# Attention weights sent between tiles on chip in 8 transfers per unit, instead of through DRAM

## The chip, the cores and the metric

The kernel runs on one core of a Trainium2 chip. The metric is the device time of one execution in microseconds (us). The kernel before took 1465.52 us, the median of three runs (1459.74 to 1465.77).

## The reference

Two blocks follow each other. The first is attention with a threshold, over 8 batches, 8 heads, 576 rows and a head size of 64, all float32. The second is a bilinear feed-forward layer over 4608 rows of 512 with 1536 hidden columns.

```python
scores = scale * np.matmul(q, k.transpose(0, 1, 3, 2))
thresh = np.max(scores, axis=-1, keepdims=True) - tau
scores = np.where(scores >= thresh, scores, -1000000000.0)
scores = scores - np.max(scores, axis=-1, keepdims=True)
attn = np.exp(scores)
attn = attn / (np.sum(attn, axis=-1, keepdims=True) + 1e-09)
out = np.matmul(attn, v)
# (B,H,S,D) -> (B*S, H*D) = x
a = x @ w_a
b = x @ w_b
return (a * b) @ w_out
```

## The kernel before

**Units.** Heads are taken in pairs: 8 batches of 4 pairs (HP = 4), 32 pairs. A pair's 576 query rows make five units: u = 0 to 3 are 128 rows for both heads, u = 4 (NT) is the tail of 64 rows, where both heads share one 128-row tile. That makes 160 units. The list `units` (L895 to L903) orders them: per batch first the units 0 and 1 of all four pairs, then 2, 3 and the tail of each; the first batch (i < HP) has its tails last.

**Slots.** The loop at L925 runs one slot per unit. In slot g TensorE computes the scores of unit g (`scores`, L340), VectorE (DVE) takes their maxima, ScalarE (ACT) the exponentials, DVE applies the threshold and sums (`weigh`), and ACT normalises (`normalise`). The result is the tile tw (three buffers): 128 partitions with query rows, and per head 576 keys in 18 blocks of 32.

**Turning the weights.** The product with v contracts over keys, so keys must lie on partitions. The first 8 units (BY_PE) are turned by TensorE (`turn_pe`). For the others DVE transposes tw in place in 32x32 blocks (`turn_blocks`, L446), in slot g + 1. After that the partition group of 32 still belongs to one block of 32 queries, and holds one key of each of the 18 key blocks, for both heads. To bring different keys to different groups, four transfers write the groups to DRAM (swap, L457), and in the slot after, `turn_back` reads it back in one transfer (L466; two at L469 for the later tails) into a tile wT, of which there are two. Partitions 0 to 63 then hold keys of the first head, 64 to 127 of the second.

**Product.** `weighted` (L539) runs for a part of a pair: units 0 and 1 (256 queries) or units 2, 3 and the tail (320 queries); in the first batch the tails are parts of their own. It runs PV_LAG = 3 slots after the part's last unit. `product` (L476) issues 36 matmuls over nine slots of keys, two row groups (one per head) by two column groups; results of a head lie crosswise in two PSUM banks, so `settle` (L487) copies one bank by ACT in one instruction and the other by DVE in two halves across partitions.

**The feed-forward layer** fills the rest of each slot: `advance` steps through its matmuls (L633, L706, L763) by a count of columns owed, `make_room` moves a product to where an accumulation ends. TensorE's instructions stand in the order of the program.

**Loads.** SyncE's queue (SP) issues nearly all transfers, in the program's order: k, q (L147) and v (L170, L172) of later pairs, weights in the first slots (L225), the swaps, and the stores of the output (L833). Eight semaphores are used in turn for its transfers, and a transfer waits for the landing of the one eight places before it.

## Time and profile before

| What | Value |
|---|---|
| median of three runs | 1465.52 us |
| profiled execution | 1467.37 us |
| its span on the core | 1465.6 us |
| TensorE clock granted | 0.994 of full |
| TensorE / DVE / ACT / GpSimd busy | 95 / 69 / 47 / 33% |
| bytes moved by DMA | 223.21 MB, 60.7% of 16 engines' time on SP's queue |
| busy of TensorE, 0 to 146.6 us | 111.2 of 146.6 us |
| busy of TensorE, 146.6 to 1330 us | 1146.9 of 1183.4 us |
| busy of TensorE, 1330 us to the end | 129.8 of 135.6 us |
| DMA share in these (first 73.3 us / to 146.6 / middle / end) | 1.06 / 0.69 / 0.66 / 0.05 |

Three stretches can be told apart. At the start loads fill the transfer engines and weights are converted. In the middle attention and feed-forward layer share the slots. After the last product, at 1330 us, only the feed-forward layer of the last rows is left. A group's line in the profile names the source line, the engine, the operation, the tiles out<-in, the shape and the count; after the bar come busy time, the mean duration of one in ns, and the idle time of the engine just before these instructions with what ended most of it. In a list of waits the numbers are us in total, times, and the longest. In a list of transfers they are the count, the size of one and the median us from issue to landing. A line of the timeline starts with start and duration in us.

### The profile page before, as it was taken

What the parts mean: (1) busy time and instruction counts of PE and PEld (TensorE: products, weight loads), DVE (VectorE), ACT (ScalarE), POOL (GpSimd) and SP (SyncE); (2) the same over time, 40 slices, a digit from 0 to 9 for tenths busy, and PEclk for the clock granted to TensorE, in tenths of its full rate; (3) what the DMA queues carried; (4) which work ended last, traced back from release to release, by engine and by line L of the source; (5) the groups of instructions that cost most, each with busy time, mean ns of one, the idle gap of its engine ahead of it and who ended that gap; (6) DMA issues with size and microseconds to landing.
All of it is one profiled execution on the core that took longest, in us unless ns stands there. A gap on an engine that the chain in (4) does not pass through costs nothing.

```text
span 1465.6 us, 76332 instructions
## 1 busy us (share of the span) xinstructions
PE 1387.9 (95%) x34208; PEld 1248.2 (85%) x34208; DVE 1014.9 (69%) x2245; ACT 682.9 (47%) x1243; POOL 479.5 (33%) x668
## 2 busy tenths in 40 slices
PE   5788999999999999999999899999999999999998
PEld 4677687987989889899998788998898979989997
DVE  6898688787767787586757677767767776755223
ACT  5787455545545554454444445444545455431110
POOL 2774713423060606033334224150606060605000
PEclk9999999999999999999999999999999999999999
DMA  9976677668756775577555766477656776450000
GB/s 217 227 207 181 155 183 190 167 169 189 195 135 160 165 203 145 137 174 180 142 135 138 163 165 169 121 177 167 173 147 144 179 188 165 122 148 30 4 17 17
DMA packets 325080, 223.21 MB, mean 152 GB/s; under 512 B 169616, under 2 KB 308880, under 8 KB 324752
## 3 DMA queue, kind: packets, MB, share of 16 engines
q1 hardware_dynamic: 322384, 217.73, 60.7%
q8 instruction: 269, 4.41, 1.3%
q10 hardware_dynamic: 2368, 0.59, 0.2%
q14 instruction: 59, 0.48, 0.1%
HBM read 128.58 MB, written 89.65 MB: 149 GB/s over the span
## 4 chain that ended last, share of the span: by engine, by line
PE 78%; DVE 7%; DMA 5%; SPq 5%; issue 3%; ACT 1%; POOL 1%; ACTq 0%; DVEq 0%; POOLq 0%
PE pab L633 24%; PE pab L706 18%; PE po L763 17%; PE pv L483 9%; PE sc L352 9%; DMA wT<-swap 2%; SPq L457 2%; DVE mx L359 2%; SPq L147 1%; DMA qT<-in_q_dram 1%; DVE tw L446 1%; DVE tw L383 1%; PE po L809 1%; SPq L225 1%; POOL kept L732 0%
## 5 line engine op out<-in xcount | busy, mean ns | idle before, releaser
L402 ACT ACTIVATE tw<-tw,rcp 128x576 f32<-128x576 f32 x272 | 197.8, 769 | 216.9 <-DVE rcp L396 216.8
L359 DVE TENSOR_REDUCE mx<-sc 128x1 f32<-128x576 f32 x288 | 205.6, 751 | 134.6 <-PE sc L352 131.3
L380 ACT ACTIVATE tw<-sc,bias,scalars 128x576 f32<-128x576 f32 x288 | 239.3, 831 | 9.8 <-DMA vm<-in_v_dram 0.2
L599 POOL TENSOR_TENSOR h<-h,u 128x512 f32<-128x512 f32 x28 | 35.1, 1272 | 621.8 <-DVE h L676 485.8
L383 DVE SCALAR_TENSOR_TENSOR tw<-sc,thr,tw 128x576 f32<-128x576 f32 x288 | 223.0, 798 | 14.0 <-ACT tw L380 13.8
L763 PE MATMUL po<-wo_sb,h 64*64 64x256 f32 x3264 | 222.9, 377 | 0.0
L352 PE MATMUL sc<-kT,qT 64*64 64x288 f32 x2016 | 192.0, 405 | 10.5 <-ACT xt L490 4.7
L446 DVE STREAM_TRANSPOSE tw<-tw 128x576 f32<-128x576 f32 x272 | 196.0, 754 | 0.8 <-ACT tw L402 0.8
L483 PE MATMUL pv<-wT,vm 64*64 64x160 f32 (+3 forms) x5184 | 182.4, 275 | 14.3 <-DMA wT<-swap 8.0
L763 PEld LDWEIGHTS po<-wo_sb,h 64*64 64x64 f32 x3264 | 167.4, 133 | 24.9
L483 PEld LDWEIGHTS pv<-wT,vm 64*64 64x64 f32 x5184 | 166.2, 135 | 25.3 <-issue 10.4
L763 PE MATMUL po<-sums_u,h 64*64 64x256 f32 x2448 | 163.9, 376 | 1.6 <-DVE h L714 1.6
L732 POOL TENSOR_TENSOR h<-h 128x256 f32<-128x256 f32 x168 | 117.4, 728 | 114.6 <-PE po L763 100.5
L352 PEld LDWEIGHTS sc<-kT,qT 64*64 64x64 f32 x2016 | 115.1, 133 | 32.5 <-ACT xt L490 12.3
L763 PEld LDWEIGHTS po<-sums_u,h 64*64 64x64 f32 x2448 | 123.4, 133 | 20.7 <-DVE h L714 2.3
L633 PE MATMUL pab<-xU,wb_sb 64*64 64x128 f32 x4096 | 133.5, 270 | 0.2 <-issue 0.2
L379 ACT ACTIVATE bias<-mx,scalars 128x1 f32<-128x1 f32 x288 | 83.0, 288 | 100.6 <-DVE mx L359 100.5
L633 PEld LDWEIGHTS pab<-xU,wb_sb 64*64 64x64 f32 x4096 | 127.6, 133 | 2.6 <-issue 0.5
L491 DVE COPY xT<-pv 64x128 f32<-64x128 f32 (+1 forms) x136 | 38.1, 280 | 120.3 <-PE pv L483 119.1
L633 PE MATMUL pab<-xS,wa_sb 64*64 64x128 f32 x2048 | 110.8, 270 | 3.2 <-POOL xS L506 2.0
L490 ACT COPY xT<-pv 128x128 f32<-128x128 f32 (+1 forms) x68 | 17.6, 258 | 206.0 <-PE pv L483 205.9
L706 PE MATMUL pab<-xS,wb_sb 64*64 64x256 f32 (+1 forms) x1536 | 99.9, 359 | 2.9 <-issue 2.9
(137 smaller groups left out, 2429.0 us busy)
## 6 DMA issues: line engine op xcount, KB each, us to landing
swap<-tw SPq DMA_DIRECT2D x480, 144.0 KB, 2.6
wT<-swap SPq DMA_DIRECT2D x120, 576.0 KB, 4.7
vm<-in_v_dram SPq DMA_DIRECT2D x128, 72.0 KB, 3.3
swap<-tw SPq DMA_DIRECT2D x128, 72.0 KB, 2.0
kT<-in_k_dram SPq DMA_DIRECT2D x112, 72.0 KB, 4.3
wT<-swap SPq DMA_DIRECT2D x56, 144.0 KB, 2.9
out_dram<-kept SPq DMA_DIRECT2D x30, 256.0 KB, 4.0
qT<-in_q_dram SPq DMA_DIRECT2D x112, 40.0 KB, 4.5
```

What stands on the lines that cost most here:

```text
L352: nc.tensor.matmul(sc[j if u < NT else 0][to, c], qT[r, q0:q0 + D], kT[r, c * SH:(c + 1) * SH], start=True, stop=True)
L359: nc.vector.tensor_reduce(mx[:, c], sc[j], axis=AX.XY, op=ALU.max)
L379: nc.scalar.activation(bias[:, j:j + 1], mx[:, j:j + 1], AF.Copy, scale=e_nscale)
L380: nc.scalar.activation(wb[j], sb[j], AF.Exp, bias=bias[:, j:j + 1], scale=e_scale)
L383: nc.vector.scalar_tensor_tensor(out=wv, in0=sb[j], scalar=thr[:, j:j + 1], in1=wv, op0=ALU.is_ge, op1=ALU.mult, accum_out=sums[:, j:j + 1])
L402: nc.scalar.activation(w, w, AF.Copy, scale=rcp[:, j:j + 1])
L446: nc.vector.transpose(w, w)
L483: nc.tensor.matmul(pv[c * D:(c + 1) * D, y], vm[rows, s], wT[y](rows, s), start=(s == 0), stop=(s == NSLOT - 1))
L633: nc.tensor.matmul(out[c * D:(c + 1) * D, r, f * P:(f + 1) * P], w[g][k][rows, w0:w0 + D], moving[k][rows], start=(fresh and k == 0 and f ...
L706: nc.tensor.matmul(pab[c * D:(c + 1) * D, r], w[rows, f // n, k, fs + c * D:fs + (c + 1) * D], moving, start=(k == 0), stop=(k == H - 1))
L732: (nc.vector if state["over"] else nc.gpsimd).tensor_tensor(*a, **kw)
L763: nc.tensor.matmul(po[c * D:(c + 1) * D, r, y], ht[rows, t0:t0 + D], other[rows, f], start=(f == 0), stop=(f == NF // 2 - 1))
```

## The change

The weights no longer pass through DRAM. `turn_blocks` only transposes; `send` then copies the transposed groups from tw straight into wT, in eight transfers per unit, one per group of 32 query rows and half of the keys. The new wT holds a whole part (two heads, up to five column groups), and there is one of it instead of two of half the size. `send_ready` holds the units that wait for it: the first unit of a part is sent only after the product of the part before has been issued, and its transfer waits for that product to have read the tile.

In the new layout a row group of 64 partitions holds keys for its own query blocks, for both heads, instead of one head for all queries. So v must lie in both row groups for both heads: `load_part` loads it once per part, in four transfers of twice the size (eight transfers with rows of 64 elements in the first batch), into one of two tiles. `load_v` stays for the first eight units. `product_of` keeps the number and shapes of the matmuls; a head's result now lies in one partition half in both banks, so that ACT copies one bank and DVE the other with one instruction each, in strides. The product runs PV_LAG = 2 slots after the part's last unit. The first eight units' turned weights use the two halves of the one wT tile.

```diff
-PV_LAG = 3
+PV_LAG = 2
...
+    def load_part(i, h):
+        b, hp = pairs[i]
+        vm = loads.tile([P, 2, NSLOT, D], FP32, tag="vm", bufs=2, name="vm")
+        vms[i, h] = vm
+        both = v[b, 2 * hp:2 * hp + 2]
+        for g in range(G):
+            to = vm[g * Q:(g + 1) * Q]
+            if i >= HP:
+                nc.sync.dma_start(to.rearrange("p j s d -> p j (s d)"),
+                                  both.rearrange("j (p c s) d -> c p j (s d)", p=Q, c=2)[g % 2])
             else:
+                for j in range(2):
+                    nc.sync.dma_start(to[:, j], both[j].rearrange("(c s p) d -> c p s d", c=2, p=Q)[g % 2])
...
     def turned_tile():
-        return work.tile([P, G + 1, NSLOT, Q], FP32, tag="wT", bufs=2, name="wT")
+        return work.tile([P, 2, G + 1, NSLOT, Q], FP32, tag="wT", bufs=1, name="wT")
...
     def turn_blocks(i, u):
         ws, _ = weights.pop((i, u))
-        t = whole.pop((i, u))
         for w in ws:
             nc.vector.transpose(w, w)
-        if u < NT:
-            swap = scratch.tile([G, P, NSLOT * Q], FP32, tag="swap", name="swap")
-        else:
-            swap = scratch.tile([2, P, NSLOT * Q], FP32, tag="swapt", name="swap")
-        swaps[i, u] = swap
+
+    def send(i, u):
+        t = whole.pop((i, u)).rearrange("p (j c s) e -> p j c (s e)", j=2, c=2)
+        wT = turned[i, 0].rearrange("p j g s e -> p j g (s e)")
         for g in range(G):
-            if u < NT:
-                to, n = swap[g], G
-            else:
-                to, n = swap[g % 2, (1 - g // 2) * D:(2 - g // 2) * D], 2
-            nc.sync.dma_start(to.rearrange("(r p) e -> p r e", p=Q),
-                              t[g * Q:(g + 1) * Q, 0:n * NSLOT].rearrange("p (r s) e -> p r (s e)", r=n))
-
-    def turn_back(i, u):
...
+            for c in range(2):
+                rows = t[g * Q:(g + 1) * Q]
+                if u < NT:
+                    r = g // 2
+                    nc.sync.dma_start(wT[(2 * r + c) * Q:(2 * r + c + 1) * Q, :, u % 2 * 2 + g % 2], rows[:, :, c])
+                else:
+                    r, j = g % 2, 1 - g // 2
+                    nc.sync.dma_start(wT[(2 * r + c) * Q:(2 * r + c + 1) * Q, j, G if i >= HP else i], rows[:, 0, c])
+
+    def send_ready():
+        while ready:
+            i, u = ready[0]
+            if (i, 0) not in turned:
+                if turned:
+                    return
+                turned[i, 0] = turned_tile()
+                for p in range(HP if u == NT else 0):
+                    turned[p, 0] = turned[i, 0]
+            send(*ready.pop(0))
...
+    def product_of(wT, vm):
+        pv = banks(wT.shape[2] * Q, "pv")
+        for s in range(NSLOT):
+            for r in range(2):
+                rows = slice(r * D, (r + 1) * D)
+                for c in range(2):
+                    nc.tensor.matmul(pv[c * D:(c + 1) * D, r], vm[rows, c, s], wT[rows, c, :, s],
+                                     start=(s == 0), stop=(s == NSLOT - 1))
+        return pv
...
     def weighted(i, h):
...
+            x = x_of[b, h][:, hp].rearrange("p (u r w) -> p u r w", u=2, r=2)
+            main = pv[:, :, 0:P].rearrange("p r (u w) -> p r u w", u=2)
+            read[0].append(nc.scalar.copy(x[:, :, 0], main[:, 0]))
+            read[1].append(nc.vector.tensor_copy(x[:, :, 1], main[:, 1]))
...
+            x = xtail_of[b // GT][:, hp, t * TAIL:(t + 1) * TAIL].rearrange("p (r w) -> p r w", r=2)
+            tail = pv[:, :, pv.shape[2] - Q:]
+            read[0].append(nc.scalar.copy(x[:, 0], tail[:, 0]))
+            read[1].append(nc.vector.tensor_copy(x[:, 1], tail[:, 1]))
...
         if g > BY_PE and g <= len(units):
             turn_blocks(*units[g - 1])
+            ready.append(units[g - 1])
+        if g > BY_PE:
+            send_ready()
...
                 weighted(*part(*units[n]))
                 running["owed"] -= NSLOT * width(*part(*units[n])) // 2
-            if BY_PE + 1 < g <= len(units) + 1:
-                turn_back(*units[g - 2])
+                done = parts.index(part(*units[n])) + 1
+            send_ready()
...
-        for p in range(1, NPR):
+        for p in range(1, HP):
             if g == first[p] - 1:
                 load_v(p)
-        if BY_PE <= g < BY_PE + HP:
-            load_v(g - BY_PE, again=True)
+        if g in (BY_PE - 1, BY_PE + 1):
+            load_part(*parts[g > BY_PE])
+        if done and done + 1 < len(parts):
+            load_part(*parts[done + 1])
```

More of the change, by code (lines that the diff above doesn't have):

```diff
@@ L122 @@
     small = pool("small", 2)
-    scratch = pool("scratch", 3, space=bass.MemoryType.DRAM)
     psum = pool("psum", 4, space=PSUM)
@@ L156, in load_rows, with load_v @@
         loaded.setdefault(i, {})[name] = room
-    def load_v(i, again=False):
+    def load_v(i):
         b, hp = pairs[i]
-        if not again:
-            loaded[i]["v"] = loads.tile([P, NSLOT, D], FP32, tag="vm", bufs=HP, name="vm")
+        if i % 2 == 0:
+            state["v"] = loads.tile([P, 2, NSLOT, D], FP32, tag="vm", bufs=2, name="vm")
+        loaded[i]["v"] = state["v"][:, i % 2]
         for j in range(2):
-            rows, half = v[b, 2 * hp + j], loaded[i]["v"][j * D:(j + 1) * D]
-            if i >= HP or again:
-                if i < HP:
-                    rows = rows.rearrange("(c s p) d -> p c s d", c=2, p=Q)
-                else:
-                    rows = rows.rearrange("(p c s) d -> p c s d", c=2, p=Q)
-                for c in range(2):
-                    nc.sync.dma_start(half[c * Q:(c + 1) * Q], rows[:, c])
-            else:
-                nc.sync.dma_start(half, rows.rearrange("(s p) d -> p s d", p=D))
+            nc.sync.dma_start(loaded[i]["v"][j * D:(j + 1) * D], v[b, 2 * hp + j].rearrange("(s p) d -> p s d", p=D))
+    def load_part(i, h):
[8 more added lines that the diff above has]
+                                  both.rearrange("j (p c s) d -> c p j (s d)", p=Q, c=2)[g % 2])
+            else:
+                for j in range(2):
+                    nc.sync.dma_start(to[:, j], both[j].rearrange("(c s p) d -> c p s d", c=2, p=Q)[g % 2])
     CW = DM
@@ L198 @@
     state = {"loaded": 0, "added": 0, "converted": 0, "rows": 0, "sums": False, "through": 0, "over": False,
-             "layer": False, "reading": False, "first": 0}
+             "layer": False, "v": None, "reading": False, "first": 0}
     NSUM = NF // 2 * 3 * CH
@@ L314 @@
     x_of, xtail_of = {}, {}
-    blocks, complete, swaps = [], [], {}
+    blocks, complete, vms, ready = [], [], {}, []
     def prep(i, name):
@@ L419, in turn_pe @@
         ws = [w.rearrange("p n e -> p (n e)") for w in ws]
-        wT = turned_tile()[:, 0:G].rearrange("p g s e -> p (g s e)").rearrange("p (s w) -> p s w", w=P)
+        if "pe" not in turned:
+            turned["pe"] = turned_tile()
+        wT = turned["pe"][:, units.index((i, u)) % 2, 0:G].rearrange("p g s e -> p (g s e)")
+        wT = wT.rearrange("p (s w) -> p s w", w=P)
         turned[i, u, "pe"] = [wT[:, :, y * D:(y + 1) * D] for y in range(2)]
@@ L443, in turn_blocks @@
         ws, _ = weights.pop((i, u))
-        t = whole.pop((i, u))
         for w in ws:
             nc.vector.transpose(w, w)
-        if u < NT:
-            swap = scratch.tile([G, P, NSLOT * Q], FP32, tag="swap", name="swap")
-        else:
-            swap = scratch.tile([2, P, NSLOT * Q], FP32, tag="swapt", name="swap")
-        swaps[i, u] = swap
-        for g in range(G):
-            if u < NT:
-                to, n = swap[g], G
-            else:
-                to, n = swap[g % 2, (1 - g // 2) * D:(2 - g // 2) * D], 2
-            nc.sync.dma_start(to.rearrange("(r p) e -> p r e", p=Q),
-                              t[g * Q:(g + 1) * Q, 0:n * NSLOT].rearrange("p (r s) e -> p r (s e)", r=n))
-    def turn_back(i, u):
-        swap = swaps.pop((i, u)).rearrange("g p e -> p g e")
-        if u < NT or i < HP:
-            turned[i, u] = turned_tile()
-            n = G if u < NT else 2
-            nc.sync.dma_start(turned[i, u][:, 0:n].rearrange("p g s e -> p g (s e)"), swap)
-        else:
-            for y in range(2):
-                nc.sync.dma_start(turned[i, 2 + y][:, G].rearrange("p s e -> p (s e)"), swap[:, y])
+    def send(i, u):
+        t = whole.pop((i, u)).rearrange("p (j c s) e -> p j c (s e)", j=2, c=2)
+        wT = turned[i, 0].rearrange("p j g s e -> p j g (s e)")
+        for g in range(G):
+            for c in range(2):
[16 more added lines that the diff above has]
+            send(*ready.pop(0))
     def join(out, lo, hi):
@@ L485, in product, with apart, settle @@
         return pv
-    def settle(out, pv, c0, c1, others):
+    def product_of(wT, vm):
[7 more added lines that the diff above has]
+        return pv
+    def apart(one, two):
+        for a in one:
+            for b in two:
+                tc.declare_no_dep(a.ins, b.ins, reason="banks of their own")
+                tc.declare_no_dep(b.ins, a.ins, reason="banks of their own")
+    def settle(out, pv, c0, c1):
         n = c1 - c0
@@ L492, in settle @@
                for c in range(2)]
-        for mine, theirs in ((one, others[1] + two), (two, others[0] + one)):
-            for a in mine:
-                for b in theirs:
-                    tc.declare_no_dep(a.ins, b.ins, reason="banks of their own")
-        others[0].extend(one)
-        others[1].extend(two)
+        apart(one, two)
     def x_tile(name):
@@ L528, in weighted_unit @@
         pv = product([lambda rows, s, t=t: t[rows, s] for t in wT], loaded[i]["v"], P)
+        if units.index((i, u)) == BY_PE - 1:
+            del turned["pe"]
         if (b, 0) not in x_of:
@@ L531, in weighted_unit @@
             state["xs"] = x_tile("xS")
-        settle(x_of[b, 0][:, hp, u * P:(u + 1) * P], pv, 0, D, ([], []))
+        settle(x_of[b, 0][:, hp, u * P:(u + 1) * P], pv, 0, D)
         exchange(x_of[b, 0], state["xs"], hp, u * P, (u + 1) * P, nc.gpsimd)
@@ L541, in weighted @@
         b, hp = pairs[i]
-        n = width(i, h)
-        if h < 2:
-            groups = G + (n > HALF)
-            wT = [turned.pop((i, 2 * h + y))[:, 0:groups] for y in range(2)]
-        else:
-            t = turned.pop((i, NT))
-            wT = [t[:, y:y + 1] for y in range(2)]
-        pv = product([lambda rows, s, t=t: t[rows, :, s] for t in wT], loaded[i]["v"], n)
+        groups = slice(i, i + 1) if h == 2 else slice(0, width(i, h) // (2 * Q))
+        wT = turned.pop((i, 0))[:, :, groups]
+        pv = product_of(wT, vms.pop((i, h)))
         read = [], []
@@ L553, in weighted @@
                 x_of[b, h] = x_tile("xT")
-            settle(x_of[b, h][:, hp, :], pv, 0, P, read)
+            x = x_of[b, h][:, hp].rearrange("p (u r w) -> p u r w", u=2, r=2)
+            main = pv[:, :, 0:P].rearrange("p r (u w) -> p r u w", u=2)
+            read[0].append(nc.scalar.copy(x[:, :, 0], main[:, 0]))
+            read[1].append(nc.vector.tensor_copy(x[:, :, 1], main[:, 1]))
             if hp == HP - 1:
                 complete.append((x_of.pop((b, h)), ("half", b, h)))
-        if n % HALF:
+        if width(i, h) % HALF:
             t = b % GT
@@ L560, in weighted @@
                 xtail_of[b // GT] = x_tile("xt")
-            settle(xtail_of[b // GT][:, hp, t * TAIL:(t + 1) * TAIL], pv, (n - TAIL) // 2, n // 2, read)
+            x = xtail_of[b // GT][:, hp, t * TAIL:(t + 1) * TAIL].rearrange("p (r w) -> p r w", r=2)
+            tail = pv[:, :, pv.shape[2] - Q:]
+            read[0].append(nc.scalar.copy(x[:, 0], tail[:, 0]))
+            read[1].append(nc.vector.tensor_copy(x[:, 1], tail[:, 1]))
             del loaded[i], prepared[i]
@@ L564, in weighted @@
                 complete.append((xtail_of.pop(b // GT), ("tail", b - t, 0)))
+        apart(*read)
     def weight_sums(n, z):
@@ L905 @@
                 if i % HP == HP - 1 and part(i, u) and (i >= HP or u == NT - 1)]
+    parts = [part(i, u) for i, u in units[BY_PE:] if part(i, u)]
     first = {i: g for g, (i, u) in enumerate(units) if u == 0}
@@ L925 @@
     for g in range(len(units) + PV_LAG):
-        written = len(pending)
+        written, done = len(pending), 0
         state["converted"] = state["added"]
```

## The prediction

> **What bounds the kernel now.** I read the page's engine line first, then its groups, then who waited for whom on TensorE's queue and on SyncE's (SP's) queue, then the issues, and last two stretches of the timeline.

> ```profile
> span 1465.6 us, 76332 instructions
> PE 1387.9 (95%) x34208; PEld 1248.2 (85%) x34208; DVE 1014.9 (69%) x2245; ACT 682.9 (47%) x1243; POOL 479.5 (33%) x668
> ...
> L483 PE MATMUL pv<-wT,vm 64*64 64x160 f32 (+3 forms) x5184 | 182.4, 275 | 14.3 <-DMA wT<-swap 8.0
> L491 DVE COPY xT<-pv 64x128 f32<-64x128 f32 (+1 forms) x136 | 38.1, 280 | 120.3 <-PE pv L483 119.1
> ```

> TensorE is the bound: the matmuls are the same in number and shape after the change (17128 in both built programs), so only its idle time, 1465.6 - 1387.9 = 77.7 us, can be won, plus whatever delays are hidden inside "busy". By stretch: 35.5 us idle up to 146.6 us, 36.5 us from there to 1330 us, 5.8 us after that. In the middle stretch TensorE idles for the weighted product (14.3 us over the run) and for the scores. These are the waits behind it:

> ```profile
> PE pv L483 <- DMA wT<-swap: 8.0, 6, 2.7
> PE pab L633 <- issue: 7.8, 14, 1.9
> ...
> PE sc L352 <- ACT xt L490: 4.7, 4, 1.2
> ...
> PE sc L352 <- DVE xt L491: 3.2, 3, 1.1
> ```

> The second resource is SP's queue, which issues nearly every transfer in order. It waited 317.7 us for the transposes and 104.8 us for products; that is its only slack, because its 1373 issues took 756 us (551 ns each with the waits inside them).

> ```profile
> SPq L457 <- DVE tw L446: 317.7, 106, 6.5
> ...
> SPq L466 <- PE pv L483: 104.8, 50, 4.7
> ```

> ```profile
> swap<-tw SPq DMA_DIRECT2D x480, 144.0 KB, 2.6
> wT<-swap SPq DMA_DIRECT2D x120, 576.0 KB, 4.7
> vm<-in_v_dram SPq DMA_DIRECT2D x128, 72.0 KB, 3.3
> swap<-tw SPq DMA_DIRECT2D x128, 72.0 KB, 2.0
> kT<-in_k_dram SPq DMA_DIRECT2D x112, 72.0 KB, 4.3
> ```

> The timeline of SP shows how dense that queue already is where k, q and v are loaded for the next pairs: from 346.70 to 361.0 us it never rests.

> ```profile
> 346.70 5.03 SPq L147 DMA_DIRECT2D kT<-in_k_dram  x4
> 351.83 2.47 SPq L457 DMA_DIRECT2D swap<-tw  x4
> 354.39 0.39 SPq L466 DMA_DIRECT2D wT<-swap  x1
> 354.88 2.08 SPq L147 DMA_DIRECT2D qT<-in_q_dram  x4
> 357.01 3.05 SPq L170 DMA_DIRECT2D vm<-in_v_dram  x4
> 360.16 0.84 SPq L833 DMA_DIRECT2D out_dram<-kept  x2
> 361.09 3.12 SPq L457 DMA_DIRECT2D swap<-tw  x4
> ```

> **The change, part by part.**

> *Old trips removed: -14.3 us.* The write to DRAM (2.6 us to land) and the read back (4.7 us) go, and with them the 14.3 us that TensorE idled at L483. What can be late next is the new transfer; it is priced separately below. Bounds: 0 (another wait ends last there) and -14.3.

> *The new transfers on SP's queue: +14 us.* A unit issues 8 transfers of 72 KB instead of 4 + 1, a part loads v in 4 transfers of 144 KB; in all 1961 issues instead of 1373. Every transfer still waits for the landing of the one eight places before it. With one wT tile, the first unit of the next part may be sent only when the running product has ended (time T). From one unit's scores to the next (a slot) the trace has 8.0 us on average (97.91 to 1302.17 us, 150 slots). After T, in a round of two units from product to product, the queue holds: 8 sends, 4 q, 4 v, 8 sends, and the next product waits for the last of these. Spacing between issues in quiet stretches: sends 0.45 us (1.76 us for four at 578.37), q 0.51 (2.03 for four), v 0.46. So 3.6 + 2.0 + 1.85 + 3.6 = 11.1 us to the end of the last issue, which began 0.35 us earlier and lands 1.75 us after its start (the four 72 KB transfers from 570.4 us landed 1.67 to 1.78 us after their starts): T + 12.5. Against it stands TensorE's work between two products in the built order. A group of four 64x128 matmuls, two passes each, takes 223 ns (866 ns for 31 weight loads in L633, so 27.9 ns each), 1.74 ns per column; the shortest rounds hold 7296 columns, 12.6 us. They are equal, so jitter decides: I take 0.5 us for each of the 11 rounds of 7296 columns or fewer in the seven later batches, 1 us for the rest (8064 columns and more give 14 us). In the first batch v goes in 8 transfers with short rows, and three tail units follow each other with 8 + 4 + 8 issues per slot, 9.5 us, where TensorE has 3360 to 4672 columns, 5.8 to 8.1 us: stalls of 2.8, 1.3 and 2.6 us, and about 1 us in the rounds before. Sum 5.5 + 1 + 7.7 = 14. Bounds: 5 (the later rounds never wait) and 37: with the medians of the page, 4.0 us for q and 3.3 and more for v, and 2.6 us for a send, the last lands at T + 14.5, so 11 rounds lose 2 us, 8 lose 0.4, the first batch 12. I stay near the lower end because 52 MB of traffic go (160 MB of swap become 80 MB, v grows by 28 MB, of 223).

> [...]

> *Scores after a wide product: -6 us.* Scores waited 7.9 us for the copies of the tail, because each head's half was copied by its own DVE instruction:

> ```profile
> 1285.33 0.59 DVE L491 COPY xT<-pv 64x128 f32<-64x128 f32 x2 [3.06 <-PE pv L483]
> 1285.93 0.39 DVE L491 COPY xt<-pv 64x32 f32<-64x32 f32 x2
> ```

> Now there is one copy each, about 0.3 + 0.2 us (ACT's 128x128 takes 266 ns) instead of 0.98. And the product falls a slot later in the pattern of units: in the built order 20 of the 28 wide products are followed by a tail unit's scores, which take one tile. Bounds 0 and -7.9.

> *Semaphores at TensorE: +6 us.* Eight landings must be waited for. The program has 391 semaphore instructions ahead of product matmuls instead of 107, up to 5 in a row; TensorE's sequencer took 51 ns for each. A single one inside a run of matmuls cost nothing (16 weight loads on each side: 846 against 903 ns in L633), so the first two of a row are free. Bounds 0 and 284 x 51 ns = 14.5; I take the middle less a little.

> *DVE and ACT: 0.* DVE saves 60 x 0.288 + 32 x 0.188 = 23.3 us of copies and gains 295 semaphores of 50 ns, 14.8 us; ACT gains 295 of 17 ns, 5 us. Both sit beside TensorE at 69% and 47%; without this cover DVE's net -8 us would still be a gain. The exp of unit g + 3 waits for the landing of unit g's sends in the same tw buffer: sent late in slot g + 1, it has over one slot left.

> *Start: +1 us.* The first two loads of v (8 transfers each, slots 7 and 9) pass ahead of weights while the transfers' share is still 0.69 to 1. An 8-transfer load is 3.7 us of issue; DVE, not TensorE, is full there (65.0 of 73.3 us). Bounds 0 and +4.

> *Instruction fetch: -2 us.* TensorE lost 17 us to "issue", which I read as late instruction loads behind other transfers; with a quarter less traffic some goes. Bounds 0 and -8.

> *A slot sooner: 0.* The FFN behind the last product is 76288 columns in both programs; the order within slots shifts, its sum does not.

> Sum: -14.3 + 14 - 6 + 6 + 1 - 2 = -1.3 us. The profiled execution took 1467.4 us, 1.9 above the median of 1465.5; against the median, **1464**.

> **Rivals.**
> *SP's queue becomes the bound (slower).* 588 more issues at 0.43 us are 253 us out of 422 us of slack, much of which can't be used, as it lies in waits for T. Place: two-unit rounds. Decides once the last send lands later than T + 13.5, 1 us past the forecast's. Price: 37 us of stalls instead of 14, sum +22: 1487; with all semaphores paid too (+8.5), 1496. For it: loads of four took 3 to 5 us at 346 to 360 us instead of 2. Against: those stood behind 576 KB reads, which go.
> *The stalls go altogether (faster).* Only the first batch waits (5 us), semaphores hide, scores gain 7.9: -14.3 + 5 - 7.9 + 1 - 2 = -18: 1447. For it: quiet landings are under 2 us. Against: the issue sum alone fills the shortest rounds.
> *The change has no visible effect on waits*: the old L483 waits sat in the same dense rounds, and reappear there. This is the forecast itself, as it comes out even.

> **How the numbers follow.** A measurement can tell about 0.5%, 7.3 us, from no change. Forecast 0.45 (own range 1452 to 1475, from jitter of 0 to 1 us per short round and 0 to 14.5 us of semaphores): faster 0.15, same 0.18, slower 0.12. SP as bound 0.30, all slower. Stalls gone 0.25: faster 0.22, same 0.03. Together faster 0.37, same 0.21, slower 0.42. The range goes from the second rival's 1447 to the first one's 1496.

> **What would show it.** At the product, TensorE's idle of 8 to 16 us ended by wT<-tw, most of it between 180 and 260 us; scores' idle down from 10.5 us to about 4; SP's wait for transposes down from 318 to some 100 us; landings of sends under 2.2 us. Wrong, if product waits exceed 30 us or sends land in 3 us (first rival), or if they stay under 5 (second), or if idle grows at a line not named here.

## The result

The changed kernel took 1737.05 us, the median of four runs (1731.68 to 1749.44); the kernel before took 1462.9 us beside it. The ratio is 1.189 (95% interval 1.181 to 1.196). The forecast was 1464 us, with a range from 1447 to 1496. The profiled execution, the slowest of the four, took 1749.44 us, its span 1747.7 us.

The lines of the changed kernel's page that answer those shown of before:

```profile
span 1747.7 us, 77662 instructions
PE 1496.1 (86%) x34208; PEld 1347.1 (77%) x34208; DVE 985.9 (56%) x2153; ACT 683.9 (39%) x1243; POOL 479.2 (27%) x668
...
PE 45%; SPq 30%; DMA 10%; DVE 9%; issue 4%; ACT 2%; POOL 0%; DVEq 0%; ACTq 0%
...
L512 PE MATMUL pv<-wT,vm 64*64 64x128 f32 (+2 forms) x4608 | 257.3, 364 | 206.9 <-DMA wT<-tw 200.6
...
L359 PE MATMUL sc<-kT,qT 64*64 64x288 f32 x2016 | 214.0, 428 | 0.9 <-DVE sums L401 0.7
...
wT<-tw SPq DMA_DIRECT2D x960, 72.0 KB, 2.1
```

TensorE executes the same 34208 matmuls. Its idle time went from 77.7 to 1747.7 - 1496.1 = 251.6 us (+173.9), and its busy time from 1387.9 to 1496.1 us (+108.2). Together that is the 282 us between the two spans. What idle was added stands at the product (L512, once 14.3 us, now 206.9 us). The last line speaks against the landing of a single transfer: 2.1 us, less than the 2.6 us of the write to DRAM before. The third line points to the place: SP's queue holds 30% of the chain that ended last. Before, that line read:

```profile
PE 78%; DVE 7%; DMA 5%; SPq 5%; issue 3%; ACT 1%; POOL 1%; ACTq 0%; DVEq 0%; POOLq 0%
```

What SP's queue waited for, from its entries for sends:

```profile
SPq L472 <- PE pv L512: 172.0, 56, 5.1
...
SPq L472 <- DMA wT<-tw: 22.0, 32, 1.4
...
SPq L472 <- DVE tw L455: 4.8, 9, 1.4
```

Before, SP waited 317.7 us for the transposes: it was ready ahead of them. Now it waits 4.8 us for them: when it comes to a send, the transposed tile is nearly always ready. What is left is the wait for the running product, which holds the one tile wT. So SP and TensorE wait for each other in turn. One round of this, from the timeline of SP and then of TensorE:

```profile
652.47 6.32 SPq L472 DMA_DIRECT2D wT<-tw  x8
658.83 2.71 SPq L146 DMA_DIRECT2D qT<-in_q_dram  x4
661.58 1.87 SPq L178 DMA_DIRECT2D vm<-in_v_dram  x4
663.55 0.37 SPq L867 DMA_DIRECT2D out_dram<-kept  x1
664.02 13.22 SPq L472 DMA_DIRECT2D wT<-tw  x10
```

```profile
662.67 2.10 PE L740 MATMUL pab<-xS,wb_sb 64*64 64x256 f32 x32
669.24 0.69 PE L512 MATMUL pv<-wT,vm 64*64 64x128 f32 x4 [4.46 <-DMA wT<-tw]
671.87 3.89 PE L512 MATMUL pv<-wT,vm 64*64 64x128 f32 x66 [1.94 <-DMA wT<-tw]
```

The product of the part before has ended at T = 652.4 us (T stands for this moment in every round). SP then issues the first unit's eight sends, q, v, a store, and the second unit's eight sends (the last group's ten are these eight and, after the next product, two of the part that follows). In each of the two groups of eight one issue took long, 1.8 and 1.7 us; the others took 0.6 us, and over the run one send began 0.64 us after the one before it in the median. The eighth of the second unit landed at 671.6 us, T + 19.2. TensorE had run out of other work at 664.8 us and waited 4.46 and 1.94 us.

What followed the waits stands in the windows of the changed kernel, each from one change of the granted clock to the next; the column after the five engines is that clock:

```profile
645.20:652.10 6.90, 4.27 (x72) 3.93 (x76) 0.00 (x0) 0.00 (x0) 0.00 (x0) 0.51 0.58 128
652.10:669.10 17.00, 12.67 (x296) 10.75 (x289) 11.45 (x26) 8.76 (x16) 0.00 (x0) 1.00 0.48 115
669.10:676.00 6.90, 4.83 (x78) 4.49 (x82) 0.00 (x0) 0.00 (x0) 0.00 (x0) 0.51 0.16 38
```

In the first and the last of these windows, which follow waits, the granted clock is 0.51, against 1.00 in the one between, and just there TensorE computes the product. The run has 47 stretches at a granted clock of 0.5, 264.7 us in all, 132 us of clock lost; before had 5, 19.5 us. TensorE was busy in 202 us of the 264.7, and half of that, 101 us against 8 before, is nearly all of the 108 us by which the same matmuls became "busier".

### The profile page after: what moved, and what is told of

Read it like the earlier page. It is cut to its first block, busy times and chain, and to the rows that moved or that the text cites. A ratio compares the mean times of both kernels' runs of the same rounds, so it can differ in the third digit from the quotient of the medians.

```text
span 1747.7 us, 77662 instructions
## 1 busy us (share of the span) xinstructions
PE 1496.1 (86%) x34208; PEld 1347.1 (77%) x34208; DVE 985.9 (56%) x2153; ACT 683.9 (39%) x1243; POOL 479.2 (27%) x668
## 2 busy tenths in 40 slices
DMA packets 289441, 171.43 MB, mean 98 GB/s; under 512 B 192848, under 2 KB 262480, under 8 KB 289104
## 4 chain that ended last, share of the span: by engine, by line
PE 45%; SPq 30%; DMA 10%; DVE 9%; issue 4%; ACT 2%; POOL 0%; DVEq 0%; ACTq 0%
SPq L472 19%; PE pv L512 12%; PE pab L667 12%; DMA wT<-tw 8%; PE po L797 7%; PE pab L740 7%; SPq L475 6%; PE sc L359 6%; DVE mx L366 3%; SPq L146 2%; SPq L178 2%; DVE tw L390 1%; DVE tw L455 1%; DVE low L267 1%; DMA qT<-in_q_dram 1%
## 5 line engine op out<-in xcount | busy, mean ns | idle before, releaser
L512 PE MATMUL pv<-wT,vm 64*64 64x128 f32 (+2 forms) x4608 | 257.3, 364 | 206.9 <-DMA wT<-tw 200.6
L512 PEld LDWEIGHTS pv<-wT,vm 64*64 64x64 f32 x4608 | 223.8, 182 | 242.7 <-issue 199.6
L633 POOL TENSOR_TENSOR h<-h,u 128x512 f32<-128x512 f32 x28 | 35.0, 1273 | 777.4 <-DVE h L710 579.2
L797 PE MATMUL po<-wo_sb,h 64*64 64x256 f32 x3264 | 232.6, 377 | 0.0
L584 DVE COPY xT<-pv 128x128 f32<-128x128 f32 x60 | 17.5, 292 | 356.1 <-PE pv L512 356.1
L359 PE MATMUL sc<-kT,qT 64*64 64x288 f32 x2016 | 214.0, 428 | 0.9 <-DVE sums L401 0.7
L797 PEld LDWEIGHTS po<-wo_sb,h 64*64 64x64 f32 x3264 | 172.9, 133 | 24.9
L583 ACT COPY xT<-pv 128x128 f32<-128x128 f32 x60 | 15.9, 265 | 443.3 <-PE pv L512 443.3
L797 PE MATMUL po<-sums_u,h 64*64 64x256 f32 x2448 | 171.6, 377 | 2.1 <-DVE h L748 2.1
L359 PEld LDWEIGHTS sc<-kT,qT 64*64 64x64 f32 x2016 | 141.6, 144 | 15.7 <-ACT xt L593 1.6
L797 PEld LDWEIGHTS po<-sums_u,h 64*64 64x64 f32 x2448 | 126.4, 133 | 22.2 <-DVE h L748 3.2
L667 PE MATMUL pab<-xT,wa_sb 64*64 64x128 f32 x1792 | 101.8, 271 | 0.8 <-DVE kept L491 0.8
## 6 DMA issues: line engine op xcount, KB each, us to landing
vm<-in_v_dram SPq DMA_DIRECT2D x232, 144.0 KB, 3.2
```

Source lines behind the costliest of these rows:

```text
L359: nc.tensor.matmul(sc[j if u < NT else 0][to, c], qT[r, q0:q0 + D], kT[r, c * SH:(c + 1) * SH], start=True, stop=True)
L512: nc.tensor.matmul(pv[c * D:(c + 1) * D, r], vm[rows, c, s], wT[rows, c, :, s], start=(s == 0), stop=(s == NSLOT - 1))
L667: nc.tensor.matmul(out[c * D:(c + 1) * D, r, f * P:(f + 1) * P], w[g][k][rows, w0:w0 + D], moving[k][rows], start=(fresh and k == 0 and f ...
L797: nc.tensor.matmul(po[c * D:(c + 1) * D, r, y], ht[rows, t0:t0 + D], other[rows, f], start=(f == 0), stop=(f == NF // 2 - 1))
```

## The experiments

The theory: the bound is SP's time for issuing. A round is a loop through one tile, product (T), eight sends, loads, eight sends, landing, product (with eight more sends where a part has three units), and SP spends 0.6 to 0.8 us on each send. Rivals: the transfers land too slowly or fill the 16 engines; each piece costs by its number; the semaphores ahead of the product; the halved clock; the wait of each transfer for the landing of the one eight places before it. The list above bounds the last: sends waited 22.0 us for landings of other sends in the whole run, of 274 us lost. "Last landing" below is worked out from each trace as the last landing of a wT transfer after the end of one product and before the end of the next, and "round" is the time between these ends; both are medians over 63 rounds, with two units or three.

| Kernel | issues on SP, us of them | last landing after T | round | time, us | ratio to before |
|---|---|---|---|---|---|
| changed | 1961, 1264 | 19.1 | 22.9 | 1737 | 1.181 to 1.196 |
| 2 sends a unit | 1049, 662 | 12.3 | 18.1 | 1444 | 0.984 to 0.990 |
| 4 sends a unit | 1353, 881 | 14.3 | 18.2 | 1465 | 0.997 to 1.005 |
| 2 sends and 6 tiny | 1961, 1282 | 20.0 | 24.3 | 1794 | 1.217 to 1.238 |
| loads behind the sends | 1961, 1254 | 17.0 | 20.1 | 1601 | 1.089 to 1.099 |

### Fewer, larger sends

```diff
-        for g in range(G):
+        for r in range(1):
+            rows = slice(r * 128, (r + 1) * 128)
             for c in range(2):
...
-                    nc.sync.dma_start(wT[(2 * r + c) * Q:(2 * r + c + 1) * Q, :, u % 2 * 2 + g % 2], rows[:, :, c])
+                    nc.sync.dma_start(wT[rows, :, u % 2 * 2 + c], t[rows, :, c])
```

> Each unit's turned weights go in 2 transfers of 288 KB over all 128 partitions instead of 8 of 72 KB (a tail unit: 2 of 144 KB). The same bytes from the same tiles into the same tiles under the same waits, but blocks of 32 partitions end up in the wrong place, so the product is of other numbers. Theory (SP's queue issues too long after the product: 8 sends, the loads, 8 sends, at 0.65 us each): a round's two units cost 4 x 0.65 = 2.6 us of issue instead of 12.6, the last send lands about 10.5 us after the product, earlier than TensorE's 12.6 us of other work, and the time falls to 1445 us (1430 to 1470), with under 15 us of idle at the product. Rival (the transfers land too slowly, or the 16 engines are full): bytes and landing are unchanged, the time stays at 1700 or more. Rival (the semaphores ahead of the product): at most 284 x 51 ns = 14.5 us go, 1735.

Measured: 1443.65 us (1442.14 to 1446.13), ratio 0.987 (0.984 to 0.990). Its page:

```profile
PE 1382.8 (96%) x34208; PEld 1255.7 (87%) x34208; DVE 986.0 (68%) x2153; ACT 683.6 (47%) x1243; POOL 480.0 (33%) x668
...
L510 PE MATMUL pv<-wT,vm 64*64 64x128 f32 (+2 forms) x4608 | 158.9, 278 | 6.0 <-PE pab L738 1.7
...
wT<-tw SPq DMA_DIRECT2D x240, 288.0 KB, 3.7
```

The loss is gone whole, although these transfers land later (3.7 us) than the small ones (2.1 us) and carry the same bytes. So neither bytes nor the time to land are the cause. This kernel leaves out the exchange of blocks between partition groups, so it gives a time and not a result to use; with the rest of the change in it, it took 19 us less than the kernel before.

With four sends a unit, over 64 partitions each (the edit against the run above):

```diff
-        for r in range(1):
-            rows = slice(r * 128, (r + 1) * 128)
+        for r in range(2):
+            rows = slice(r * 64, (r + 1) * 64)
```

> 4 transfers of 144 KB over 64 partitions for each unit, between the 8 of the changed kernel and the 2 tried before; blocks of 32 partitions end up in the wrong place, so the product is of other numbers, at the same bytes and waits. Theory (the queue of SP, which turns into a bound when its issues after the product outlast TensorE's round): 608 x 0.67 = 407 us of issue go, the last send lands about 2.7 + 4.7 + 2.7 + 2.4 = 12.5 us after the product, against 12.6 us of TensorE's work, so nearly all of the loss goes: 1455 us (1442 to 1480). Rival (each transfer costs its share, whatever the queue's slack): halfway by count, 1444 + 305 x 2 / 6 = 1545.

Measured: 1464.93 us (1460.13 to 1475.10), ratio 1.001 (0.997 to 1.005). Twice the sends of the run above cost 21 us, twice again 272 us: a threshold, which fits a queue that fills up, and not a price per transfer (which would have given 1545 us).

### SP's time alone

Both runs above took pieces, semaphores and issues away at once. Here the issues come back without the pieces (the edit against the kernel with two sends).

```diff
             for c in range(2):
+                for k in range(6 * c):
+                    at = state["tiny"] = (state["tiny"] + 1) % 48
+                    nc.sync.dma_start(spare[0:Q, at:at + 1], scalars[0:Q, 0:1])
```

> The kernel with 2 sends a unit, and between the two 6 transfers of 4 bytes in each of 32 partitions into a spare tile that nothing reads: 8 issues a unit on SP as in the changed kernel, but the wT bytes still land in 2 transfers (with blocks in the wrong place, so the product is of other numbers), and TensorE has 2 landings a unit to wait for instead of 8. Theory (SP's time for issues alone): a tiny transfer takes SP about 0.6 us too, 912 of them 547 us, the last send lands 18 us after the product instead of 12.3, and the loss comes back: 1690 us (1600 to 1760). Rival (bytes in small pieces, slow landings or semaphores at TensorE): 1444 to 1465, as without the tiny ones.

Measured: 1794.09 us (1790.86 to 1797.33), ratio 1.227 (1.217 to 1.238). Its page:

```profile
L514 PE MATMUL pv<-wT,vm 64*64 64x128 f32 (+2 forms) x4608 | 251.6, 382 | 259.0 <-DMA wT<-tw 185.1
...
wT<-tw SPq DMA_DIRECT2D x240, 288.0 KB, 3.1
...
spare<-scalars SPq DMA_DIRECT2D x912, 0.1 KB, 2.1
```

Transfers of 128 bytes in all, which TensorE needs for nothing, bring the loss back whole, and more. Their issue took 0.590 us in the median (0.686 in the mean), the same as for 72 KB (0.596 and 0.686). The number of landings that TensorE has to wait for is that of the fast kernel, and the two real sends landed sooner than there (3.1 against 3.7 us). This settles it: SP's time for issuing makes the loss.

### The order on SP

```diff
+    later = []
...
         if g > BY_PE:
             send_ready()
+        while later:
+            later.pop(0)()
...
-                    load(p, name)
+                    later.append(lambda p=p, name=name: load(p, name))
...
-            load_part(*parts[done + 1])
+            later.append(lambda x=parts[done + 1]: load_part(*x))
```

> The loads of q, k and v are issued after the sends of the following unit instead of ahead of them; all else as in the changed kernel. Theory: after the product SP issues 8 + 8 sends back to back (12.6 us) and the last lands 14.6 us after the product instead of 19; the round is then set by SP's sum of issues (12.6 sends + 5 loads + 0.5 store, about 18 us) instead of the 23 us seen, so 1540 us (1490 to 1600), and SP waits for next to nothing. Rival (landing or the engines' rate): 1740 or more, since neither count nor bytes change. Rival (the sum of SP's issues alone sets the pace already now): no change either, 1740.

Measured: 1600.78 us, ratio 1.094 (1.089 to 1.099). The count, the bytes and the engines are unchanged, and 136 us come back: the place in the queue counts. From the timeline of SP and from its waits:

```profile
608.85 2.10 SPq L146 DMA_DIRECT2D qT<-in_q_dram  x4
610.99 1.87 SPq L178 DMA_DIRECT2D vm<-in_v_dram  x4
612.97 12.96 SPq L472 DMA_DIRECT2D wT<-tw  x16
625.98 2.13 SPq L146 DMA_DIRECT2D qT<-in_q_dram  x4
```

```profile
SPq L472 <- PE pv L512: 56.0, 28, 4.2
```

The queue hardly rests any more: it waits 56.0 us for the product instead of 172.0, and issues alone fill 84 to 92 us of each 100 from 100 to 1400 us. At 1601 us it came out at the far end of what was expected. In the seven later batches the rounds of two units went as expected: 17.6 us, the last landing 14.7 us after T (medians). The expectation had no sum for the rounds of three units, which are as many. There loads still stand ahead of the third unit's eight sends, the last one lands 22.2 us after T, and the round takes 25.4 us. What a second wT tile would give, so that sends need not wait for the product, no run tried.

### The kernel before with as many transfers

```diff
-            nc.sync.dma_start(to.rearrange("(r p) e -> p r e", p=Q),
-                              t[g * Q:(g + 1) * Q, 0:n * NSLOT].rearrange("p (r s) e -> p r (s e)", r=n))
+            for c in range(2):
+                m = n // 2
+                nc.sync.dma_start(to[c * m * Q:(c + 1) * m * Q].rearrange("(r p) e -> p r e", p=Q),
+                                  t[g * Q:(g + 1) * Q, c * m * NSLOT:(c + 1) * m * NSLOT].rearrange("p (r s) e -> p r (s e)", r=m))
```

> The kernel before, with each write of a unit to DRAM cut in two: 8 writes instead of 4, 1981 issues on SP instead of 1373, about as many as in the changed kernel (1961). Theory (what hurts is the loop product, sends, loads, sends, product through one tile, with 0.65 us for each send between tiles): here writes wait for no product, and cost 0.43 us; 608 x 0.43 = 261 us of issue go into 422 us of SP's waits, and the time rises by 5 to 50 us, to about 1485. Rival (the number of transfers is what the chip charges, wherever they go and whatever waits): as bad as the changed kernel, 1650 to 1750.

Measured: 1556.64 us (1554.85 to 1560.11), ratio 1.064 (1.062 to 1.067). Neither theory had this. The number alone costs 93 us, a third of the loss, even where the added transfers wait for no product: SP has 1065 us of issue instead of 756, and what reads back stands behind it. On the page:

```profile
L485 PE MATMUL pv<-wT,vm 64*64 64x160 f32 (+3 forms) x5184 | 203.6, 293 | 78.2 <-DMA wT<-swap 62.0
```

It counts for the theory that 1981 issues of the shorter kind (0.427 us in the median) cost far less than 1961 with the longer one through the loop.

### The halved clock

Extra matmuls on weights that lie there anyway fill TensorE's wait ahead of the product, in 20 groups and, with `range(8)`, in 8.

```diff
+        for f in range(20):
+            for r in range(2):
+                rows = slice(r * D, (r + 1) * D)
+                for c in range(2):
+                    nc.tensor.matmul(pv[c * D:(c + 1) * D, r], wa_sb[rows, 0, 0, 0:D], wa_sb[rows, 0, 1, 0:pv.shape[2]],
+                                     start=True, stop=True)
```

> Ahead of each product TensorE gets 20 x 4 matmuls of two weight tiles that have long been there into the same bank, overwritten by the product: about 4.5 us of work in the place where it now waits for the sends. Theory (a wait also costs the halved granted clock after it, which stretches the product that the next sends wait for): the granted clock stays at 1.0 in most rounds, the product's busy time falls from 257 us towards the 182 us of before, and the time falls by 40 to 90 us, to about 1680. Rival (the wait alone counts, the halved clock falls on work that would wait anyway): 1745, or more by what the extra matmuls overshoot.

> As with the 20 extra groups of matmuls ahead of each product, but 8 groups: by the 20 groups' 326 us, about 130 us of extra work over the run, less than the 207 us that TensorE waits there. Theory (the halved clock after a wait stretches the product, and with it the round): idle at the product falls to 80 to 120 us, waits get too short to halve the clock in most rounds, and the time falls by 40 to 100 us, to about 1680. Rival (the round is set by SP alone, the halved clock costs nothing): 1740 to 1760, the extra work taking the place of idle.

Measured: 1793.49 us (ratio 1.221 to 1.230) with 20 groups and 1763.43 us (1.200 to 1.206) with 8, so 56 and 26 us more than the changed kernel where the theory had 40 to 100 us less. The page of the first:

```profile
PE 1697.0 (95%) x44448; PEld 1586.6 (89%) x44448; DVE 982.4 (55%) x2153; ACT 683.9 (38%) x1243; POOL 481.0 (27%) x668
...
L512 PE MATMUL pv<-wa_sb 64*64 64x128 f32 (+2 forms) x10240 | 326.3, 279 | 16.2 <-DVE tw L390 14.8
...
L518 PE MATMUL pv<-wT,vm 64*64 64x128 f32 (+2 forms) x4608 | 172.1, 285 | 30.8 <-DMA wT<-tw 29.5
```

The clock did what was meant: 0.991 granted in the mean instead of 0.925, and the product is down from 257 to 172 us. The time didn't follow; the extra matmuls are 326 us of work in place of 207 us of idle. The last landing stays at 19.7 us (20 groups) and 19.6 us (8 groups) after T, against 19.1: SP paces the round, and the clock isn't what starts the loss. What the halved clock adds to it isn't settled: with 20 groups the median round shrank from 22.87 to 22.36 us, while the mean grew from 23.7 to 24.3 us. The next sends wait for the product's end, so a slower product lengthens the round. Over the whole run the product's busy time was 85 us shorter here than in the changed kernel, and 98 us shorter with two sends a unit. As an estimate from these, the halved clock added up to that much on this path; how much is open.

### A second queue

The same eight sends, part of them or the loads from another engine's queue.

```diff
             for c in range(2):
+                engine = (nc.sync, nc.scalar)[c]
...
-                    nc.sync.dma_start(wT[(2 * r + c) * Q:(2 * r + c + 1) * Q, :, u % 2 * 2 + g % 2], rows[:, :, c])
+                    engine.dma_start(wT[(2 * r + c) * Q:(2 * r + c + 1) * Q, :, u % 2 * 2 + g % 2], rows[:, :, c])
```

> Half of the sends (those of the second half of the keys) are issued from ACT's queue instead of SP's; the same 8 transfers of the same bytes, the same waits, the loads stay ahead of the next unit's sends on SP. Theory (one queue issues one transfer after the other): SP's sum of issues falls from 1264 us to about 850, a unit's sends leave in 2.7 us instead of 5.4, the last one lands about 13 us after the product instead of 19, and the time falls to 1490 us (1450 to 1540); ACT pays 608 x 0.65 = 395 us of issue at 39% busy, and its exp waits behind sends that wait for the product. Rival (the chip charges the number of small transfers, whichever queue issues them): 1700 or more. Rival (ACT, blocked by sends that wait, becomes the next bound): 1550 to 1650, with exp late and TensorE waiting for scores' banks.

> Both at once: half of the sends from ACT's queue, and the loads behind the following unit's sends. Theory: after the product SP issues 4 + 4 sends (5.3 us), the last lands about 8 us after it, well ahead of TensorE's 12.6 us; no idle at the product, 1450 us (1438 to 1480), so about as fast as with 2 sends a unit. Rival (ACT as the next bound): 1500 or more, and no better than with half of the sends on ACT alone. Rival (the number of transfers): 1600, as with the order alone.

Measured: 1857.06 us (ratio 1.261 to 1.272), and with the loads behind the sends 1875.48 us (1.276 to 1.282), the slowest kernels of all. In the first of them the last landing came to 15.6 us after T and TensorE's idle at the product fell to 11.5 us, so SP's part went as the theory has it, though later than its 13 us. But ACT's own work now stood behind the sends. From the page of this kernel, the waits of ACT and those of TensorE:

```profile
L513 PE MATMUL pv<-wT,vm 64*64 64x128 f32 (+2 forms) x4608 | 167.2, 280 | 11.5 <-issue 5.0
```

```profile
ACT bias L386 <- DMA wT<-tw: 232.7, 45, 8.1
...
ACT tw L409 <- DMA wT<-tw: 109.1, 37, 3.9
```

```profile
PE sc L359 <- DVE tw L390: 82.5, 56, 8.0
```

The exponentials came late, with them the threshold, and TensorE waited for the scores' banks (82.5 us for DVE's threshold, 2.9 us in the changed kernel). The third expectation, ACT as the next bound, had the mechanism, at a higher price than it said. The next run gives ACT only half of the later units' sends, behind the exponentials, with the loads behind the sends on SP:

```diff
+        later_half = u in (1, 3) or (u == NT and i >= HP)
...
+                if later_half and c:
+                    others.append(move)
+                else:
+                    nc.sync.dma_start(*move)
...
+            nc.scalar.dma_start(*others.pop(0))
...
         if here:
             weigh(i, u)
+        send_others()
```

> Loads behind the following unit's sends, and half of the sends of a part's later units alone from ACT, placed behind the exps of the next unit, so that none of them waits for the product or for a transpose any more. Theory (ACT failed because it stood waiting with exp behind it): SP's issues after the product are 8 + 4, 8.1 us, landing 10.2 us after it; no idle at the product, ACT's issues of about 0.69 us delay each normalise by 2.8 us in every second slot: 1470 us (1445 to 1520). Rival (ACT's issue time itself is what delayed scores): 1600 or more, with TensorE waiting at the scores for DVE's threshold as in the run with half of all sends on ACT.

Measured: 1552.20 us (ratio 1.046 to 1.075), 323 us less than with half of all sends on ACT and the same order, but not the 1470 us expected. ACT's issues took 0.71 us each, and normalise still waited 121.0 us for sends. The next runs used POOL, whose issues took 0.50 to 0.67 us. First half of each unit's sends, with the loads behind the sends on SP, then all sends of the later units (with the loads in their old place, and behind the sends), then the loads instead of sends:

```diff
+                engine = (nc.sync, nc.gpsimd)[c]
```

```diff
+        engine = nc.sync if u in (0, 2) else nc.gpsimd
```

```diff
-                nc.sync.dma_start(to.rearrange("p j s d -> p j (s d)"),
+                nc.gpsimd.dma_start(to.rearrange("p j s d -> p j (s d)"),
...
-                    load(p, name)
+                    later.append(lambda p=p, name=name: load(p, name, nc.gpsimd))
```

> Half of the sends from GpSimd's (POOL's) queue, loads behind the following unit's sends. No run has shown what POOL takes for an issue. Theory (SP's queue was the bound, ACT failed because exp and normalise stood behind its sends): POOL's own work is exchanges and sums that have slack (27 to 33% busy), so sends may block it: if an issue takes POOL 1 us or less, 1450 us (1438 to 1490). Rival (POOL blocked by sends that wait for the product makes the exchanges late, on which the next FFN block waits): 1550 or more.

> All 8 sends of each part's later units (and of the tail units) from GpSimd's (POOL's) queue, the first unit's 8 from SP, the loads in their old place. Unlike with half of every unit's sends on POOL, POOL's queue no longer holds sends that wait for the running product (247 us of its waits there). Theory (SP's queue was the bound, and the two trials with another queue lost by blocking that engine's own work): SP keeps about 835 us of issues, POOL takes 640 x 0.53 = 340 us; the last send lands about 10 us after the product, ahead of TensorE's 12.6: 1452 us (1440 to 1480). Rival (8 small transfers a unit cost by their number, whichever queue): 1530 or more, as with half of each unit on POOL. Rival (POOL's exchanges and sums stay late behind sends that wait for transposes): 1500 to 1540, with TensorE waiting for xS and h.

> The same with the loads a slot later on SP. Theory: SP has nothing behind the loads that is due, so the order no longer matters: within 6 us of the same kernel with the loads in their old place. Rival (SP still late for the first unit's sends, because loads stand ahead of them): 10 to 20 us slower, since the loads now stand closer to the next product's end.

> All 8 sends of each unit stay on SP; the loads of q, k and v of the attention batches go from POOL's queue, a slot later than before, so that none waits for the running product. Theory: SP has 1216 sends (823 us) and little else, after the product 16 sends back to back, the last landing 16 x 0.72 + 1.7 = 13.2 us after it, near TensorE's 12.6: 1490 us (1455 to 1530), POOL paying 400 x 0.53 = 212 us. Rival (POOL's queue takes the loads too late, or its own sums become late): TensorE waits for qT, vm or xS, 1540 or more. Rival (order and queue make no difference beyond the order alone): 1601.

Measured: 1536.63, 1590.81, 1597.12 and 1543.23 us (ratios 1.041 to 1.059, 1.081 to 1.090, 1.083 to 1.094, 1.047 to 1.065). All four beat the changed kernel by 140 to 200 us, and none comes near 1450. The place of the loads made 6 us between the second and the third, as expected. The blocking that they were meant to avoid came in another form. From the waits on POOL's queue, first of the kernel with the later units' sends on POOL, then of the one with the loads there:

```profile
POOL wT L473 <- DMA wT<-tw: 308.1, 29, 15.5
```

```profile
POOL vm L178 <- PE pv L512: 263.3, 29, 22.8
```

In the first POOL stood for landings of other sends, with its exchanges and sums behind it; in the second v still waited for the product. With the loads on POOL SP had little but sends and stores in the middle stretch, yet its sends landed in 3.4 us instead of 2.1 and the last one 16.3 us after T; why the landing got slower there was not tried. So in these runs a second queue relieved SP, and each cost something of its own: with half of all sends on ACT the exponentials' bias and normalise waited 232.7 and 109.1 us for them; POOL's queue stood 308.1 us for other sends with the later units' sends there, and 263.3 us for the product with the loads there.

### The product a slot sooner

The kernel with two sends a unit, with the old lag:

```diff
-PV_LAG = 2
+PV_LAG = 3
```

> The kernel with 2 sends a unit, with the product a slot later again (three units behind the scores, as in the kernel before) and all else the same. The forecast's step says that a slot sooner is worth nothing: 1444 us, within 4 us of the kernel with 2 sends. Rival (the sooner product is what gains, by ending the scores' wait or by shortening the last stretch): 1455 to 1465.

Measured: 1489.66 us (1484.07 to 1493.10), ratio 1.015 (1.012 to 1.018), against 0.987 at two slots. The change's own lag is worth 46 us here between the medians, 41 us by the two ratios, more than the 11 to 21 us of the rival. From the waits of SP's queue, with two slots and with three, and of ACT with three:

```profile
SPq L471 <- PE pv L510: 218.1, 57, 5.9
```

```profile
SPq L471 <- PE pv L510: 500.8, 56, 16.4
```

```profile
ACT tw L387 <- DMA wT<-tw: 100.2, 47, 5.5
```

With one tile, a product a slot later holds the next part's sends a slot longer (SP waits 500.8 instead of 218.1 us for it), and the exponential of three units on needs the buffer that these sends have yet to read. That these waits make up the whole difference isn't shown.

## Why the prediction was wrong

**The step that failed is "The new transfers on SP's queue: +14 us"**, and in it three inputs.

*The issue of a send, 0.45 us.* It was read from the writes to DRAM (0.433 us in the median), the nearest row, taken for the same thing. A send from tile to tile has 0.596 us in the median and 0.686 us in the mean, and the eight of a unit took 6.3 us in the round shown, one long issue of 1.8 us among them, not 3.6. Both bounds of the step varied landings and the duration of loads; neither varied this. With 6.3 + 2.7 + 1.9 + 0.4 + 6.2 and the landing of the last one the round shown gives T + 19.2 instead of T + 12.5. The first rival decided "once the last send lands later than T + 13.5", and that is what happened; its price, 37 us of stalls, was the same sum with the same 0.45 us in it.

*The rounds of three units.* Where the step had 14 us of idle at the product, the run had 206.9: 22.3 us in the first batch (7.7 in the step), 94.4 us at the 28 products that follow two units in the later batches, and 90.2 us at the 28 that follow three. These last the step had taken to be safe, with 1 us for all rounds over 7296 columns; but they hold 24 sends, and the last one landed 23.6 us after T (median).

*The sum over the run.* The first rival set 588 more issues at 0.43 us, 253 us, against 422 us of SP's waits. Measured, SP's issues went from 756 to 1264 us, +508 us: sends 823.1 instead of 400.9 us for the old writes and reads (+422), v 165 instead of 73 us (+93), k and q 14 us less, the rest 7 us more. That is more than the slack. About 1166 us of the issues lie between 146.6 us and the last product. At the highest density that the loads behind the sends reached, 92 us in 100, these would need some 1270 us, where the kernel before took 1183: by this estimate neither order tried could have held the old pace. The step counted only the excess in number, though each replaced write had become dearer too.

**The price of a stall** was its own length in this sum. In the trace the halved clock followed the stalls, and busy time grew by 108 us. By how much the run was longer for it isn't shown.

**Old trips removed, -14.3 us, and scores after a wide product, -6 us.** Right in direction and about in size, as seen where nothing else hides them: with two sends a unit the product's idle is 6.0 us and that of the scores 1.6 us (10.5 before). The second rival's 1447 us, which has 5 us of stalls in it, came within 3 us of that kernel's 1444; since that is another kernel, it bears out the terms and not the rival. DVE's copies of the main columns took 292 ns each, as assumed (about 0.3 us).

**Semaphores at TensorE, +6 us.** Their size wasn't measured by itself. With two landings to wait for instead of eight, and SP's issues kept, the loss was not smaller, so they can't be what made it.

**A slot sooner, 0.** Wrong: it looked at the feed-forward layer's columns alone, but the lag also sets when the one tile comes free (46 us with two sends a unit). The changed kernel has the shorter lag, so this didn't add to the loss.

**Start, instruction fetch, DVE and ACT: +1, -2 and 0.** No run tells these apart. That TensorE's 17 us of "issue" were late instruction loads was the author's estimate.

**What would show it.** "Product waits exceed 30 us" was the line drawn for the first rival: 206.9 us. The line "sends land in 3 us" would have led astray: they landed in 2.1 us, as forecast (under 2.2), and the loss came all the same. Traffic fell from 223.21 to 171.43 MB, as forecast, and brought nothing that these runs can show.

**Issue against landing.** The step set an issue of 0.45 us beside a landing of 1.75 us. That transfers overlap is what the traces show: in the kernel before, four writes of 72 KB had landed 3.1 us after the first one's start (at 570.40 us), 1.67 to 1.78 us each. In the changed kernel sends began 0.64 us apart (median) and landed 2.1 us after their issue, several in flight. Here the issuing queue's time was the bound: a send held it for 0.69 us in the mean, and the 1961 issues of this one queue took 1264 us.

## What to carry to other kernels

Before transfers are split or added, sum what the issuing queue spends on them, kind by kind, against the time that the queue has, and lay out one round from the event that frees the buffer to the last landing; the median landing (2.1 us here, against the last one at T + 19.1) tells nothing of either. Take the issue time from a row of the same kind of transfer (here 0.60 us between tiles, 0.43 us from a tile to DRAM), and where there is none, let it vary in the bounds. Transfers moved to a compute engine's queue stood ahead of that engine's own work in the runs on ACT and POOL: of these seven none came back to the old time (1536.63 to 1875.48 us against 1465.52), and those with half of all sends on ACT were the slowest (1857.06 and 1875.48 us).
